# An attention, low-rank mix and MLP kernel on one core: float32 in the low-rank part, an earlier decode of two weight blocks, and the last first-layer products one part ahead

## The chip, the cores and the metric

The kernel runs on one core of a Trainium2 chip. The metric is device time in microseconds (us) of one execution; of the kernel before, three runs were timed, and a fourth execution was profiled. The engines are PE (TensorE matmuls; PEld are its weight loads), DVE (VectorE), ACT (ScalarE), POOL (GpSimd) and SP, which issues DMAs.

## What is computed

```python
# attention: batch 4, 12 heads, 448 tokens, head size 64
scores = q @ k.T / 8, causal mask, softmax
x = softmax @ v                      # (4, 448, 768)
# low-rank mix over the tokens, rank 32
u = x + ((x.T @ U) @ V).T            # U (448, 32), V (32, 448)
# MLP, 768 -> 3072 -> 768
out = u + relu(u @ w_ch1) @ w_ch2
```

The weights U, V, w_ch1 and w_ch2 come as float64 and are turned into float32 on the chip ("decoded").

## The kernel before, in words

Everything is held transposed: features on the partitions, tokens along the columns. There are three stages.

**Attention** (span 0 to about 152 us alone, then mixed with the next stage). A plan (`PLAN`, L47) lists the steps of a head with a lag each; iteration n does, in the plan's order, the scores of head n (tile `s`, L214), the transposes of its probabilities (`t`, L266) two iterations later, the product with v for each two heads (`pv`, L281), and so on. ACT takes exp (L242) and copies transposes out of PSUM (L167), DVE the row maxima (L228), POOL the normalising (L255). The instruction order in this stage and the next is the order in which the code is written (`manual_schedule`).

**The low-rank part** follows for each two heads: x is transposed back (`xt`, L311) and split into a high part, rounded to fp32r by ACT (`xn_h`, L315), and a low part, the rest, by DVE (`xn_l`, L320). For each four heads `low_rank` (`y`, L328) multiplies four tiles of 112 tokens with U: eight fp32r matmuls of 256 columns, with the high and low parts of U side by side in 128 weight columns (`um_s`). ACT copies the high part of y out (L337), DVE the low part (L341). `mix` (`hm`, L346 and L347) multiplies y with the high and the low part of V, two fp32r matmuls of 448 columns, for each of the six feature chunks of a batch; the mixes of batch 0 stand in iterations 14 to 19, those of batch 1 in 26 to 31. `mix_sum` (L351) adds on DVE. For batches 0 and 1 POOL then splits u into high and low parts (L171, L175). There are 12 `y` groups and 24 `hm` pairs in all: `y` in iterations 8, 12, ... 52.

**Decode.** A block of weights (128 x 768 float64, 768 KB) is loaded by SP (`load_w`) and decoded in three steps: step 0 has two ACT instructions (L152, L156) and three on DVE (L153 to L155), step 1 one on POOL (L160) and a DMA that keeps the result in HBM, step 2 a copy on ACT (L178) and a subtraction on DVE (L179). Blocks 0 and 1 are loaded in iterations 10 and 11 and decoded in iterations 26 to 32 (`W_AT` counts back from `START` = 34); U and V are loaded after iteration -1 and decoded in iterations 3, 5 and 6 (`VU_AT`).

**MLP of batches 0 and 1** (152 to 580 us): `hf` (L415) and `of` (L440), in groups of 9 fp32r matmuls, with the rest of attention, the low-rank steps and the decode of the other blocks put between them.

**MLP of batches 2 and 3** (580 us to the end): a Strassen scheme with 7 products for each quad of weight blocks, all at L647, in six parts p. A part has the first-layer quads (1, p, 0) and (1, p, 1), 63 matmuls each, and three second-layer quads (2, p, k), 42 each; a pair (q, n) in the code is product n of quad q, in PSUM banks `sa`, `sb` and `se`. When a first-layer quad is done, `hidden` turns its result r into seven operands with high and low parts (`h`): for each of r's halves and sums ACT rounds to the high part (L469) and DVE subtracts (L461). Second-layer results are added to x by DVE (`xb<-sa` and so on, L461). The order of the products is written by hand (`seq`); within it a scheduler places the instructions of this stage on the engines. Tiles `uch` and `ucl` hold the operands of the first layer to the end.

Of the kernel before, what the change touches and what calls it, by code (L numbers as in the profile page):

```python
# [69 lines left out]
def attention_mix_mlp(ctx: ExitStack, tc: tile.TileContext, qk, v, w1, w2, vu, out):  # L70
# [42 lines left out]
    um_s = const.tile([CP, NT, 4, R], F32R, name="um_s")  # L113
    vm_h = const.tile([P, S], F32R, name="vm_h")
    vm_l = const.tile([P, S], F32R, name="vm_l")
    xn_h = const.tile([CP, NT, 2 * P], F32R, name="xn_h")
    xn_l = const.tile([CP, NT, 2 * P], F32R, name="xn_l")
# [63 lines left out]
    def low_rank_weights(step):  # L181
        if step == 0:
            st["vu"] = load_words(vu, VCOLS)
        elif step == 1:
            st["vua"] = decode_bits(st["vu"], VCOLS)
        elif step == 2:
            decode_sum(st.pop("vu"), st["vua"], VCOLS)
        else:
# [1 line left out]
            split(a[:, :S], vm_h, vm_l)  # L190
            u = a[:CP, S:].rearrange("p (s r) -> p s r", s=NT)
            for i in (0, 2):
                split(u, um_s[:, :, i, :], um_s[:, :, i + 1, :])
# [539 lines left out]
    for p in range(NPART):  # L733
# [4 lines left out]
        else:  # L738
            order((b, 0), (b, 1), (k2, 5), (b, 2), (b, 3), (b, 4))
        if p + 1 < NPART:  # L740
# [3 lines left out]
            order((k1, 0), (k1, 3))  # L744
        else:
            order((b, 5), (b, 6), (k0, 0, 0), (k0, 3, 0), (k0, 1, 0), (k1, 0, 0), (k1, 3, 0), (k1, 1, 0))
            order((k0, 0, 1), (k0, 3, 1), (k0, 2), (k0, 1, 1), (k0, 6), (k0, 4), (k1, 0, 1), (k1, 3, 1))
        order((k0, 5), (k1, 2))
        order(*([(k1, 1)] if p + 1 < NPART else [(k1, 1, 1)]), (k1, 6), (k1, 4))
# [229 lines left out]
```

## Time and profile before

| | |
|---|---|
| runs | 911.19, 913.18, 915.44 us; median 913.18 us |
| profiled execution | 909.54 us, of it span 907.6 us |
| PE busy in the span | 877.9 us, 97% |
| DVE, ACT, POOL busy | 663.6, 486.6, 314.4 us (73%, 54%, 35%) |
| chain that ended last | PE 78%, DVE 10%, ACT 7% |

The profile page shows one execution; its views by stretches, by groups of instructions and in order of time are shown below. A matmul's record lasts longer than the array is held by it, since matmuls are pipelined: the price of a group is read from its start to the start of what follows.

### The profile page before, as it was taken

To read this page: it belongs to the slowest core of one execution; us is meant where nothing else is said; L and a number is where in the kernel's file an instruction comes from. 1 tells how busy PE (TensorE), PEld (TensorE's weight loads), DVE (VectorE), ACT (ScalarE), POOL (GpSimd) and SP (SyncE) were. 2 spreads that over 40 slices of the span, in tenths; PEclk is the share of its full clock that TensorE was granted. 3 is DMA by queue.
4 is the path that set the end of the run, shared out by engine and by line. 5 is a ranking of instruction groups with operands and counts; after the bars stand their busy time and mean duration, and the time that the engine had idled before them with its cause. 6 is when DMAs were issued, how large, how long until landed. Compare 5 with 4: busy or idle time off the path is not lost.

```text
span 907.6 us, 13761 instructions
## 1 busy us (share of the span) xinstructions
PE 877.9 (97%) x4728; PEld 749.6 (83%) x4728; DVE 663.6 (73%) x1320; ACT 486.6 (54%) x1050; POOL 314.4 (35%) x342
## 2 busy tenths in 40 slices
PE   6999998999999999999999999899999998999998
PEld 4776766888888888878889999898999897898987
DVE  4656677565665756657568788789888988989885
ACT  5998987654555544455444545364453634445350
POOL 3547576221222322223214425323424323322420
PEclk9999999999999999999999999999999999999999
DMA  8584565354454455433434446612211321202103
GB/s 209 135 216 128 151 156 155 125 174 139 135 179 134 157 165 163 139 116 119 153 105 156 157 157 208 203 42 71 70 52 35 94 59 42 72 24 85 47 1 122
DMA packets 51285, 110.02 MB, mean 121 GB/s; under 512 B 5392, under 2 KB 26896, under 8 KB 51216
## 3 DMA queue, kind: packets, MB, share of 16 engines
q1 hardware_dynamic: 51216, 109.14, 39.7%
q8 instruction: 38, 0.62, 0.3%
q14 instruction: 31, 0.25, 0.1%
HBM read 84.74 MB, written 24.38 MB: 120 GB/s over the span
## 4 chain that ended last, share of the span: by engine, by line
PE 78%; DVE 10%; ACT 7%; issue 3%; DMA 1%; POOL 1%; SPq 0%; DVEq 0%; ACTq 0%; POOLq 0%
PE hf L415 20%; PE of L440 19%; PE sa L647 14%; PE se L647 6%; PE s L214 5%; PE pv L281 5%; PE t L266 4%; ACT p L242 3%; PE sb L647 3%; DVE h L461 2%; DVE tmp L461 2%; DVE sw L461 1%; DVE wsp L461 1%; PE y L328 1%; DVE p L228 1%
## 5 line engine op out<-in xcount | busy, mean ns | idle before, releaser
L440 PE MATMUL of<-g,wsp 128*128 128x448 f32 x864 | 183.8, 368 | 0.0
L461 POOL TENSOR_TENSOR wsp<-wld,wsp 128x512 fp32r<-128x512 f32 (+1 forms) x60 | 104.1, 1745 | 219.2 <-ACT wsp L584 113.2
L440 PEld LDWEIGHTS of<-g,wsp 128*128 128x128 f32 x864 | 160.2, 188 | 18.3 <-issue 2.1
L160 POOL TENSOR_TENSOR wa<-wld 128x768 int32<-128x768 int32 (+1 forms) x49 | 73.2, 1494 | 289.0 <-issue 159.6
L242 ACT ACTIVATE p<-p,m 112x448 f32<-112x448 f32 x192 | 99.7, 523 | 59.6 <-DVE m L228 59.3
L255 POOL TENSOR_SCALAR p<-p,r 112x448 f32<-112x448 f32 x192 | 96.7, 521 | 67.7 <-DVE r L250 40.5
L647 PE MATMUL sa<-h,wsp 128*128 128x448 f32 x432 | 98.5, 367 | 1.4 <-DVE xb L461 0.7
L647 PE MATMUL sa<-uch,wsp 128*128 128x448 f32 x288 | 89.6, 371 | 7.5 <-ACT r L668 4.8
L415 PE MATMUL hf<-u,wsp 128*128 128x448 f32 x432 | 94.9, 370 | 0.0
L415 PE MATMUL hf<-wsp 128*128 128x448 f32 x432 | 94.0, 368 | 0.5 <-ACT pt L167 0.5
L228 DVE CUSTOM_DVE_ANT_0 p<-s,mask 112x448 f32<-112x448 f32 x192 | 75.8, 443 | 20.0 <-PE s L214 19.1
L443 DVE TENSOR_TENSOR xa<-of,xa 128x448 f32<-128x448 f32 x96 | 58.7, 619 | 42.9 <-PE of L440 42.3
L647 PEld LDWEIGHTS sa<-h,wsp 128*128 128x128 f32 x432 | 80.7, 188 | 9.9 <-DVE xb L461 2.0
L415 PEld LDWEIGHTS hf<-u,wsp 128*128 128x128 f32 x432 | 79.8, 188 | 10.7 <-issue 3.8
L415 PEld LDWEIGHTS hf<-wsp 128*128 128x128 f32 x432 | 80.0, 188 | 9.9 <-issue 0.9
L424 DVE SCALAR_TENSOR_TENSOR g<-hf,g 128x448 fp32r<-128x448 f32 x48 | 29.9, 623 | 71.9 <-ACT g L423 71.8
L214 PE MATMUL s<-qk 64*112 64x448 f32 (+3 forms) x384 | 70.5, 444 | 6.6 <-DMA qk<-in_qk_dram 4.2
L178 ACT CAST wsp<-wa 128x768 fp32r<-128x768 f32 x48 | 40.0, 833 | 68.4 <-POOL wa L160 50.9
L423 ACT ACTIVATE g<-hf 128x448 fp32r<-128x448 f32 x48 | 26.1, 543 | 84.0 <-PE hf L415 83.8
L167 ACT COPY pt<-t 112x336 f32<-112x336 f32 x144 | 62.1, 472 | 10.7 <-PE t L266 10.7
L647 PEld LDWEIGHTS sa<-uch,wsp 128*128 128x128 f32 x288 | 54.0, 188 | 16.2 <-ACT r L668 8.3
L584 ACT CAST wsp<-wld 128x512 fp32r<-128x512 f32 (+1 forms) x60 | 41.7, 703 | 47.1 <-PE sa L647 35.7
(92 smaller groups left out, 1598.4 us busy)
## 6 DMA issues: line engine op xcount, KB each, us to landing
wld<-in_w_dram SPq DMA_DIRECT2D x48, 768.0 KB, 4.7
qk<-in_qk_dram SPq DMA_DIRECT2D x96, 224.0 KB, 4.1
kept<-wa SPq DMA_DIRECT2D x48, 384.0 KB, 2.6
wld<-kept SPq DMA_DIRECT2D x24, 384.0 KB, 3.3
wld<-kept SPq DMA_DIRECT2D x72, 128.0 KB, 2.5
v<-in_v_dram SPq DMA_DIRECT2D x24, 224.0 KB, 4.8
out_dram<-xa SPq DMA_DIRECT2D x12, 224.0 KB, 2.3
out_dram<-xb SPq DMA_DIRECT2D x12, 224.0 KB, 1.9
```

The costliest lines, as they stand in the source:

```text
L160: nc.gpsimd.tensor_tensor(a.bitcast(I32), t[:, :n, 1].bitcast(I32), t[:, :n, 0].bitcast(I32), op=ALU.add)
L167: nc.scalar.copy(o, i)
L214: nc.tensor.matmul(o[:, : (i + 1) * CP], t[r, 0, i * CP : (i + 1) * CP], t[r, 1, : (i + 1) * CP], start=True, stop=True,)
L228: nc.vector.tensor_tensor_reduce(out=st["p", b, h][:, POFF[i] : POFF[i] + n], in0=st.pop(("o", b, h, i))[:, :n], in1=mask[:, S - n :], sca ...
L242: nc.scalar.activation(pi, pi, AF.Exp, bias=m[:, i : i + 1], scale=-1.0, accum_out=l[:, i : i + 1])
L255: nc.gpsimd.tensor_scalar(pi, pi, r[:, i : i + 1], 1.0, op0=ALU.mult, op1=ALU.mult)
L281: nc.tensor.matmul(o[j * D : (j + 1) * D, kt * CP : S], v[:, kt, j, :], pt[:, n0 : n0 + S - kt * CP], start=(kt == 0), stop=(kt == NT - 1),)
L415: nc.tensor.matmul(o, a[:, cs], m, start=(kc + n == 0), stop=(kc + n == NC + 1))
L440: nc.tensor.matmul(o, a[:, cs], m, start=(fc + n == 0), stop=(fc + n == FC + 1))
L443: nc.vector.tensor_tensor(x, o, x, op=ALU.add)
L461: (nc.vector if e == "V" else nc.gpsimd).tensor_tensor(o, a, b, op=op)
L647: nc.tensor.matmul(st[bank, q], a, b, start=(n in FIRST and ms[0] == 0 and k == 0), stop=(n in LAST and end and k == len(steps) - 1), skip ...
```

## The change

Three things are changed.

1. The low-rank part is float32 throughout. U, V, x and y have no low parts: two DVE copies in place of three splits, `natural_low` (DVE, 24 instructions) and `low_rank_low` (DVE, 12) are gone, and `y` has 32 rows. `low_rank` has four float32 matmuls of 256 columns with 32 weight columns in place of eight fp32r ones, `mix` one float32 matmul of 448 columns over 32 rows in place of two fp32r ones over 128 rows. A float32 matmul of the code is two instructions in a trace: the program has two `pv` products of 448 columns for each two heads, the trace four.
2. U and V are loaded after iteration 1 and decoded in iterations 4 to 6; blocks 0 and 1 are loaded in iterations 3 and 5 and decoded in iterations 8 to 13.
3. In the Strassen stage the quad (1, 5, 1) of the last part is multiplied in part 4, among that part's second layer. Both first-layer quads of part 5 then go through `hidden` at the end of part 4, into tiles that held `uch` and `ucl`; part 5 has second-layer products alone. The last quad's results are stored as each is ready in the code's order.

```diff
-VU_AT = (-1, 3, 5, 6)
+VU_AT = (1, 4, 5, 6)
-W_AT = (8, 6, 4, 3, 2)
+W_AT = (8, 9, 10, 11, 13)
...
     def low_rank(b, n):
         if n == 0:
-            st["y", b] = p_y.tile([P, DM], F32R, tag="y", name="y")
-        o = st["yo", b, n] = bank("y")[:, : 2 * P]
+            st["y", b] = p_y.tile([R, DM], F32, tag="y", name="y")
+        o = st["yo", b, n] = bank("y")[:R, : 2 * P]
         for s in range(NT):
-            for t in (xn_h, xn_l):
-                nc.tensor.matmul(
-                    o,
-                    um_s[:, s].rearrange("p a r -> p (a r)"),
-                    t[:, s, :],
-                    start=(s == 0 and t is xn_h),
-                    stop=(s == NT - 1 and t is xn_l),
-                )
...
+            nc.tensor.matmul(o, um[:, s], xn[:, s, :], start=(s == 0), stop=(s == NT - 1))
...
-    def low_rank_low(b, n):
-        y, o = st["y", b][D:, n * 2 * P : (n + 1) * 2 * P], st.pop(("yo", b, n))
-        nc.vector.tensor_tensor(y, o[D:], f(y), op=ALU.subtract)
...
     def mix(b, c):
         o = st["h", b, c] = bank("hm")[:, :S]
-        ys = st["y", b][:, c * P : (c + 1) * P]
-        nc.tensor.matmul(o, ys, vm_h, start=True, stop=False)
-        nc.tensor.matmul(o, ys, vm_l, start=False, stop=True)
+        nc.tensor.matmul(o, st["y", b][:, c * P : (c + 1) * P], vm, start=True, stop=True)
...
         def operand(key):
+            if q[1] == NPART - 1:
+
+                if not last:
+                    last.extend(p_uc.tile([P, 7, S], F32R, tag=f"u{x}{k}", name="h") for x in "hl")
...
+        if p + 2 == NPART:
+
+            b2 = (1, p + 1, 1)
+            order((a2, 0), (b, 5), (a2, 1), (b, 6), (a2, 2), (a2, 3))
+            order((k0, 0, 0), (k0, 3, 0), (a2, 4), (k0, 1, 0), (a2, 5), (k0, 0, 1), (k0, 3, 1), (a2, 6))
+            order((k0, 2), (k0, 1, 1), (b2, 0), (k0, 4), (b2, 1), (k0, 6), (b2, 2), (k0, 5), (b2, 3), (b2, 4))
+            order((k1, 0), (b2, 5), (k1, 3), (b2, 6), (k1, 2), (k1, 1), (k1, 6), (k1, 4))
...
-                    if q[0] == 2 and q[2] == NC // 2 - 1 and q[1] + 1 < NPART:
+                    if q[0] == 2 and q[2] == NC // 2 - 1 and q[1] + 2 < NPART:
                         layer.extend(hidden((1, q[1] + 1, 0)))
+                    elif q == (1, NPART - 1, 1):
+                        layer.extend(hidden((1, NPART - 1, 0)) + hidden(q))
...
-        early += [(10, load_w, (0,)), (11, load_w, (1,))]
+        early += [(3, load_w, (0,)), (5, load_w, (1,))]
```

On PE, iteration 16: the scores, `y`, `xt` and `hm`. Before:

```order
L214 MATMUL s<-qk 112x224
L328 MATMUL y<-xn_h,um_s 128x256
L328 MATMUL y<-xn_l,um_s 128x256
L328 MATMUL y<-xn_h,um_s 128x256
L328 MATMUL y<-xn_l,um_s 128x256
L328 MATMUL y<-xn_h,um_s 128x256
L328 MATMUL y<-xn_l,um_s 128x256
L328 MATMUL y<-xn_h,um_s 128x256
L328 MATMUL y<-xn_l,um_s 128x256
L311 MATMUL xt<-ident,xa 112x128 x4
L346 MATMUL hm<-vm_h,y 128x448
L347 MATMUL hm<-vm_l,y 128x448
```

And now, in the same iteration:

```order
L210 MATMUL s<-qk 112x224
L318 MATMUL y<-xn,um 32x256 x4
L307 MATMUL xt<-ident,xa 112x128 x4
L325 MATMUL hm<-vm,y 128x448
L262 MATMUL t<-ident,p 112x112 x10
```

The places stay; eight matmuls have become four, and two have become one.

On ACT, step 0 of the decode of block 0 (the two rows from `wld`) stands between a head's exps and its copies. Before, in iteration 26:

```order
L242 ACTIVATE p,l<-p,m 112x448
L242 ACTIVATE p,l<-p,m 112x336
L242 ACTIVATE p,l<-p,m 112x112
L242 ACTIVATE p,l<-p,m 112x224
L152 ACTIVATE wa<-wld 128x768
L156 ACTIVATE wld<-wld 128x768
L167 COPY xa<-pv 128x448
L167 COPY pt<-t 112x336
```

Now, in iteration 8:

```order
L238 ACTIVATE p,l<-p,m 112x448
L238 ACTIVATE p,l<-p,m 112x336
L238 ACTIVATE p,l<-p,m 112x112
L238 ACTIVATE p,l<-p,m 112x224
L150 ACTIVATE wa<-wld 128x768
L154 ACTIVATE wld<-wld 128x768
L165 COPY xa<-pv 128x448
L165 COPY pt<-t 112x336
```

The two instructions stand at the same place of an iteration that is 18 earlier.

On DVE, the work around the last `hidden`. Before, in part 5, where (1, 5, 1) is turned into operands:

```order
L461 TENSOR_TENSOR r<-se,r 128x448
L461 TENSOR_TENSOR h<-r,h 128x448
L461 TENSOR_TENSOR tmp<-r 128x896
L461 TENSOR_TENSOR r<-se,r 128x448
L461 TENSOR_TENSOR h<-tmp,h 128x896
L461 TENSOR_TENSOR tmp<-r,tmp 128x448 x2
L461 TENSOR_TENSOR h<-r,h 128x896
L461 TENSOR_TENSOR xb<-se,xb 128x448
L461 TENSOR_TENSOR h<-tmp,h 128x896
L461 TENSOR_TENSOR xb<-sa,xb 128x448
L461 TENSOR_TENSOR xb<-sb,xb 128x448
L461 TENSOR_TENSOR wsp<-sw,wsp 128x512
```

Now, at the end of part 4, in the middle of the two quads (1, 5, 0) and (1, 5, 1):

```order
L439 TENSOR_TENSOR tmp<-r,tmp 128x448
L439 TENSOR_TENSOR xb<-se,xb 128x448
L439 TENSOR_TENSOR xb<-sa,xb 128x448
L439 TENSOR_TENSOR h<-tmp,h 128x896
L439 TENSOR_TENSOR h<-r,h 128x896
L439 TENSOR_TENSOR tmp<-r 128x896
L439 TENSOR_TENSOR xb<-sa,xb 128x448
L439 TENSOR_TENSOR h<-r,h 128x448
L439 TENSOR_TENSOR h<-tmp,h 128x896
L439 TENSOR_TENSOR xb<-se,xb 128x448
L439 TENSOR_TENSOR tmp<-r,tmp 128x448
L439 TENSOR_TENSOR xb<-sa,xb 128x448
```

Before, one quad's operands stand there with one addition between them; now two quads' operands follow each other, with the additions of part 4's second layer between them. From the first `h<-r,h 128x896` of the two quads to the addition that the last product of part 4, n = 5 of (2, 4, 2), waits for (it frees bank `sa`), DVE's order has 27 rows: six `h` of 896 columns, two `h` of 448, one `tmp<-r` of 896 columns, four `tmp<-r,tmp`, eleven additions to `xb`, one to `r` and two weight steps (`wsp<-sw`). In the same stretch PE's order has 91 matmuls between the last one of (1, 5, 1) and that product.

## Rows read from the trace of the kernel before

**Rows 1.** Busy time by stretches: start and end in us, length, then busy us and instructions of PE, PEld, DVE, ACT and POOL, the granted clock of PE, DMA share and GB/s. Iterations 8 to 13, the MLP stage with attention in it, and the last part.

```profile
35.37:59.84 24.47, 24.20 (x187) 19.07 (x185) 14.12 (x67) 22.66 (x75) 11.57 (x24) 1.00 0.76 201
...
152.00:470.00 318.00, 315.98 (x1699) 264.44 (x1700) 196.61 (x402) 159.25 (x327) 80.97 (x98) 1.00 0.45 142
...
861.00:907.60 46.60, 41.00 (x195) 35.67 (x193) 33.29 (x54) 13.44 (x24) 8.61 (x6) 0.99 0.16 60
```

**Rows 2.** The same view by pairs of iterations, each from one `pv` group to the next: two pairs of batch 0 with mixes in them, two of batch 1 with mixes and decode, and what follows.

```profile
59.84:68.69 8.85, 8.79 (x63) 6.37 (x61) 5.55 (x25) 8.26 (x28) 4.79 (x10) 1.00 0.72 161
...
77.80:86.45 8.65, 8.58 (x61) 5.79 (x60) 5.51 (x24) 7.58 (x25) 6.97 (x13) 1.00 0.52 133
...
110.52:121.42 10.90, 9.03 (x62) 6.35 (x61) 8.15 (x28) 9.85 (x30) 6.08 (x10) 1.00 0.44 118
...
130.53:141.42 10.89, 8.84 (x61) 5.82 (x61) 8.85 (x23) 9.03 (x26) 8.65 (x16) 1.00 0.65 148
141.42:152.00 10.58, 10.34 (x66) 6.89 (x65) 8.32 (x27) 7.57 (x26) 7.46 (x10) 0.84 0.55 170
```

**Rows 3.** PE in order of time in iteration 16: start, length, line, operation, tiles, shape.

```profile
72.96 0.39 PE L328 MATMUL y<-xn_h,um_s 112*128 112x256 f32 x1
...
74.02 0.60 PE L311 MATMUL xt<-ident,xa 128*112 128x128 f32 x4
74.38 0.45 PE L346 MATMUL hm<-vm_h,y 128*128 128x448 f32 x1
...
74.87 1.12 PE L266 MATMUL t<-ident,p 112*112 112x112 f32 x10
```

**Rows 4.** PE in order of time in the MLP stage, around the last low-rank groups.

```profile
440.84 0.28 PE L328 MATMUL y<-xn_h,um_s 112*128 112x256 f32 x1
...
441.80 2.00 PE L415 MATMUL hf<-wsp 128*128 128x448 f32 x9
...
454.47 2.09 PE L415 MATMUL hf<-u,wsp 128*128 128x448 f32 x9
456.40 0.60 PE L311 MATMUL xt<-ident,xb 128*112 128x128 f32 x4
...
457.25 2.01 PE L415 MATMUL hf<-u,wsp 128*128 128x448 f32 x9
459.10 0.36 PE L346 MATMUL hm<-vm_h,y 128*128 128x448 f32 x1
...
459.50 1.99 PE L415 MATMUL hf<-wsp 128*128 128x448 f32 x9
...
468.44 0.44 PE L346 MATMUL hm<-vm_h,y 128*128 128x448 f32 x1 [1.53 <-DVE y L341]
```

**Rows 5.** PE groups by line and shape in the first 150 us: count, busy us, mean ns of one.

```profile
L281 PE MATMUL pv<-pt,v 112*64 112x448 f32 x60 | 18.1, 584 | 1.4 <-ACT pt L167 1.2
...
L281 PE MATMUL pv<-pt,v 112*64 112x112 f32 x60 | 7.8, 268 | 0.0
...
L328 PE MATMUL y<-xn_l,um_s 112*128 112x256 f32 x28 | 7.0, 281 | 0.0
...
L347 PE MATMUL hm<-vm_l,y 128*128 128x448 f32 x12 | 4.4, 366 | 0.0
```

**Rows 6.** DVE in order of time at the last `y` of the kernel: the subtraction that `hm` of Rows 4 waits for.

```profile
467.86 0.43 DVE L341 TENSOR_TENSOR y<-y 64x256 fp32r<-64x256 f32 x1
```

**Rows 7.** ACT groups by line and shape between 110.52 and 141.42 us: the decode's instructions.

```profile
L156 ACT ACTIVATE wld<-wld 128x768 int32<-128x768 uint32 x2 | 1.8, 909 | 0.0
L152 ACT ACTIVATE wa<-wld 128x768 f32<-128x768 f32 x2 | 1.8, 888 | 0.0
...
L178 ACT CAST wsp<-wa 128x768 fp32r<-128x768 f32 x1 | 0.8, 818 | 0.0
```

**Rows 8.** DVE in order of time: one decode instruction in iteration 30.

```profile
133.65 2.50 DVE L179 TENSOR_TENSOR wsp<-wa,wsp 128x768 fp32r<-128x768 f32 x1
```

**Rows 9.** DVE and ACT groups by line and shape from 809 to 905 us, the last two parts.

```profile
L461 DVE TENSOR_TENSOR xb<-sa,xb 128x448 f32<-128x448 f32 x25 | 15.4, 620 | 6.1 <-PE sa L647 6.0
L461 DVE TENSOR_TENSOR h<-tmp,h 128x896 fp32r<-128x896 f32 x8 | 11.8, 1479 | 1.5 <-ACT h L469 1.5
...
L461 DVE TENSOR_TENSOR tmp<-r,tmp 128x448 f32<-128x448 f32 x8 | 6.4, 797 | 0.6 <-DVE tmp L461 0.5
L461 DVE TENSOR_TENSOR h<-r,h 128x896 fp32r<-128x896 f32 x3 | 4.3, 1436 | 0.0
...
L461 DVE TENSOR_TENSOR tmp<-r 128x896 f32<-128x896 f32 x3 | 3.2, 1082 | 0.0
L461 DVE TENSOR_TENSOR h<-r,h 128x448 fp32r<-128x448 f32 x4 | 3.2, 795 | 1.2 <-ACT h L469 1.2
...
L469 ACT CAST h<-r 128x896 fp32r<-128x896 f32 x3 | 2.8, 944 | 0.0
```

**Rows 10.** PE in order of time in part 5: its two longest stops.

```profile
873.87 0.36 PE L647 MATMUL sa<-uch,wsp 128*128 128x448 f32 x1
875.00 0.47 PE L647 MATMUL se<-uch,wsp 128*128 128x448 f32 x1 [0.77 <-DVE r L461]
...
879.78 0.37 PE L647 MATMUL se<-h,wsp 128*128 128x448 f32 x1
880.81 0.47 PE L647 MATMUL sa<-h,wsp 128*128 128x448 f32 x1 [0.66 <-ACT h L469]
```

More of the change, by code (lines that the diff above doesn't have):

```diff
@@ L112, in attention_mix_mlp @@
     mask = const.tile([CP, S], F32, name="mask")
[L113 to L117, printed above, removed]
+    um = const.tile([CP, NT, R], F32, name="um")
+    vm = const.tile([R, S], F32, name="vm")
+    xn = const.tile([CP, NT, 2 * P], F32, name="xn")
     def f(ap):
@@ L189, in low_rank_weights @@
             a = f(st.pop("vua"))
[L190 to L193, printed above, removed]
+            nc.vector.tensor_copy(vm, a[:R, :S])
+            nc.vector.tensor_copy(um, a[:CP, S:].rearrange("p (s r) -> p s r", s=NT))
     def load_qk(b, h):
@@ L641, in product @@
             else:
-                bh, bl = st["H", m][j]
+                bh, bl = st["H", q[1], m][j]
             cs = slice(m * P, (m + 1) * P)
@@ L696, in hidden @@
         ops = [None] * 7
+        last = []
         def operand(key):
+            if q[1] == NPART - 1:
+                if not last:
+                    last.extend(p_uc.tile([P, 7, S], F32R, tag=f"u{x}{k}", name="h") for x in "hl")
+                h, l = (t[:, UPOS[key]] for t in last)
+                for n in [2] if key == "o" else range(UPOS[key].start, UPOS[key].stop):
+                    ops[n] = last[0][:, n], last[1][:, n]
+                return h, l
             if key == "o":
@@ L712, in end @@
         def end():
-            st["H", k] = ops
+            st["H", q[1], k] = ops
             used.add(("H", q[1], k))
@@ L743, in attention_mix_mlp @@
             order((a2, 5), (k0, 0, 1), (k0, 3, 1), (a2, 6), (k0, 2), (k0, 1, 1), (k0, 6), (k0, 4))
-            order((k1, 0), (k1, 3))
+            order((k1, 0), (k1, 3), (k0, 5), (k1, 2), (k1, 1), (k1, 6), (k1, 4))
         else:
[L746 to L749, printed above, removed]
+            order((k0, 0), (k0, 3), (k2, 5), (k0, 2), (k0, 1), (k0, 6), (k0, 4), (k1, 0), (k1, 3))
+            order((k0, 5), (k1, 2), (k1, 1), (k1, 6), (k1, 4))
         order((k3, 0), (k3, 3), (k1, 5), (k3, 2), (k3, 1), (k3, 6), (k3, 4))
@@ L759, in attention_mix_mlp, with stored @@
             units.append(g)
-    def stored(q):
+    def stored(q, n):
         if q[0] == 2 and q[1] == NPART - 1:
-            for d in range(2):
-                for b in range(2):
-                    nc.sync.dma_start(
-                        out=out[2 * q[2] + d, :, (b + 2) * S : (b + 3) * S], in_=xs(q, d, b)
-                    )
+            for d, b in {1: ((0, 0),), 4: ((1, 1),), 5: ((0, 1),), 6: ((1, 0),)}.get(n, ()):
+                nc.sync.dma_start(
+                    out=out[2 * q[2] + d, :, (b + 2) * S : (b + 3) * S], in_=xs(q, d, b)
+                )
     loaded, prepared = [0], [0]
@@ L820, in strassen @@
                 results(q, n)
+                stored(q, n)
                 used.add((q, n))
@@ L853, in attention @@
             "lv": load_v, "v": values, "vc": values_out,
-            "xp": x_natural, "xh": natural_high, "xl": natural_low,
+            "xp": x_natural, "xh": natural,
         }
-        by_four = {"lp": low_rank, "lh": low_rank_high, "ll": low_rank_low}
+        by_four = {"lp": low_rank, "lh": low_rank_out}
         todo = []
@@ L897, in attention_mix_mlp @@
         ):
-            early += [(START - n, step, a) for step, a in steps]
+            early += [(n, step, a) for step, a in steps]
+        early.sort(key=lambda e: e[0])
         todo = attention()
```

17 lines of the change are left out of this document (6 added, 11 removed), and 4 rows, old and new, of the table PLAN.

## The prediction

> **What bounds the kernel now.** I read the stretches first [rows 1]. From 152 to 470 us PE is busy 315.98 of 318.00 us: whatever is added to PE there is paid in full, and whatever leaves DVE (196.61 us busy) or ACT (159.25 us) brings nothing unless PE was waiting for it. In iterations 8 to 13 PE is busy 24.20 of 24.47 us, but ACT stands at 22.66 us, so two engines are near the end of their time. In the last part DVE has 33.29 of 46.60 us and PE stops for short waits. Next the pairs of iterations [rows 2]: with two mixes and no decode a pair takes 8.85 and 8.65 us, with decode 10.90 and 10.89 us at the same PE work, and the stretch behind it runs at a mean granted clock of 0.84, that is, in part at 1.2 GHz instead of 2.4 GHz; before it, PE had stopped several times. Then single groups, start to start, for prices [rows 3, 4].
>
> **Part 1, float32.** What is removed on DVE (36 subtractions) is off the path but for one place: the last `y` is subtracted only at 467.86 us [rows 6], behind a decode's DVE work, and PE waits 1.53 us for it [rows 4]. That wait goes: -1.5 us. What is late next there is ACT's copy of y, which was long done.
>
> What is added is PE time. A float32 product is two instructions. Per instruction, the `pv` groups of 448 and 112 columns last 584 and 268 ns, which is 316 / 336 = 0.94 ns a column with the queueing in it; fp32r, with 366 ns at 448 columns and 281 ns at 256, takes 85 / 192 = 0.44 ns [rows 5]. 0.44 ns is about one column in a cycle at 2.4 GHz (0.417 ns). I take float32 as two cycles, 0.83 ns, for each of the two instructions: it lies below the 0.94 ns that hold some waiting for the neighbour head, and the lower bound is 0.44 ns, if the narrow shapes (32 weight columns, 32 rows) ran as fp32r does.
>
> - `y` after: 4 products x 2 instructions x 256 columns x 0.83 = 1.71 us (0.90 to 1.93). Before: 74.02 - 72.96 = 1.06 us in attention [rows 3], 441.80 - 440.84 = 0.96 us in the MLP stage [rows 4].
> - `hm` after: 2 x 448 x 0.83 = 0.75 us (0.39 to 0.84). Before: 74.87 - 74.38 = 0.49 us [rows 3], 459.50 - 459.10 = 0.40 us [rows 4].
> - A group of nine fp32r matmuls takes 456.40 - 454.47 = 1.93 us behind a float32 group and 459.10 - 457.25 = 1.85 us behind an fp32r one [rows 4]: 0.08 us more for what stands behind each new float32 group.
>
> From 152 us on there are 5 `y` and 12 `hm`: 5 x 0.75 + 12 x 0.35 + 17 x 0.08 = 9.3 us, less the 1.5 us: **+7.8 us**. In attention there are 7 `y` and 12 `hm`. The `hm` stand in iterations 14 to 19 and 26 to 31, where PE sets the pace: 12 x 0.26 = 3.1 us. Of the `y`, those of iterations 8 and 12 fall where ACT will set the pace (part 2) and are counted at nothing; if ACT has room they cost 0.65 us each. The other five: 3.3 us. Together **+6.4 us**. Both come to +14.2 us.
>
> The price of a column is the number on which this rests, so I set the skill beside it. In the rows one product costs 2 x 0.83 = 1.67 ns a column against 0.44 ns, 3.8 times. The Trainium skill, page "FP8 and Floating Point Precision", section "TensorE Precision Notes", says that true FP32 is four passes through the array. By that rule a column costs 4 x 0.44 = 1.76 ns and the 23,040 columns of all `y` and `hm` products 2 us more than in my sum; the trace agrees that the change's float32 is not free.
>
> **Part 2, the decode.** In its old place it cost (10.90 + 10.89) - (8.85 + 8.65) = 4.3 us [rows 2], and behind it the half clock: the `pv` group at 141.42 us belongs to the stretch at 0.84, whose missing 0.16 x 10.58 us is 1.7 us [rows 2]. Both go: -6.0 us. In its new place each step 0 adds two ACT instructions of about 0.9 us, and one copy of 0.82 us belongs to it: 2 x 1.8 + 0.8 = 4.4 us [rows 7], queued behind a head's exps and ahead of the copies that `t`, `pv` and PE wait for. ACT had 24.47 - 22.66 = 1.8 us of idle time there [rows 1], so the stretch grows by 2.6 us at least and 4.4 us at most; I take 3.5 us. On DVE and POOL the place is better: in iteration 30 a subtraction took 2.50 us [rows 8] while POOL was splitting u, and POOL does no splitting in iterations 8 to 13. SP is passed by two loads of 768 KB earlier than before; in iterations 8 to 13 the two loads stood in a DMA share of 0.76 without stopping PE [rows 1], so I cost them at nothing; if the loads of q and k behind them come late, it is the few us of a landing. U and V one iteration later in the decode: nothing, the same ACT work. Sum **-2.5 us** (-6.0 to +2).
>
> **Part 3, the last part.** It removes the wait for (1, 5, 1) in part 5. PE's two stops there are 875.00 - 873.87 and 880.81 - 879.78 us, each less the 0.2 us of a matmul: 0.92 + 0.82 = 1.7 us [rows 10]. It adds, at the end of part 4, two quads' operands in a row. DVE's order there has, from the first `h` to the addition that frees bank `sa` for part 4's last product, 6 `h` of 896 columns (2 x 1.44 + 4 x 1.48 = 8.8 us), 2 `h` of 448 (1.6), one `tmp<-r` (1.1), four `tmp<-r,tmp` (3.2), 12 additions of 0.62 (7.4) and two weight steps at about the same (1.2): 23.3 us [rows 9]. It can't begin before ACT's first cast of 0.94 us [rows 9], and that waits until PE has read the tiles `uch` for the last time. So the addition ends some 24.2 us after the last first-layer matmul. PE has 91 matmuls in that time, at 1.85 / 9 = 0.206 us each [rows 4]: 18.7 us. PE waits the difference, 5.5 us, in several stops, each at an addition that stands behind an `h`. Net **+3.8 us** (-1.7 if the stops vanish, +6 if DVE is slowed by POOL besides). The stores gain nothing: one of them waits for the last addition either way.
>
> **Sum.** 7.8 + 6.4 - 2.5 + 3.8 = +15.5 us. Against the profiled execution's 909.54 us that is 925.0 us; the median of the runs lies 3.6 us higher, at 913.18 us, and I forecast for it **928.7 us**, slower by 1.7%.
>
> **The rivals.**
>
> - *Float32 at fp32r's rate.* If an instruction of these narrow shapes takes 0.44 ns a column, the 46,080 columns of all instructions save 0.39 x 46,080 = 18.0 us: 910.7 us, no change. Against it: `pv`, with 64 weight columns, is narrow too and pays 0.94 ns.
> - *The narrow products run beside their neighbours* (the one on the other side). They take 12 x 1.71 + 24 x 0.75 = 38.5 us of PE. If more than 20.1 us of that lay beside other matmuls, the kernel would be faster by over 0.5%; with all of it hidden, 928.7 - 38.5 = 890 us. Against it: next to them stand `t`, `xt`, `hf` and `of` on 112 or 128 rows [rows 3, 4], which leave no rows free, and their own instructions use the same rows. The Trainium skill, page "TensorE: Matmul & The Clock Gate", section "Why this matters for your kernels", says that a matmul of 32 rows alone takes as long as one of 128 and that the gain lies in running it beside others in other row groups. No run here shows that for these shapes.
> - *Part 4 covers the operands.* PE's stops of 5.5 us don't come: 923.2 us. For it: a part holds two `hidden` of some 7.9 us of DVE each [rows 9] all along, and most of that is covered. Against it: DVE's order, counted above.
> - *The decode is free in its new place*: 925.2 us. For it: ACT idles 1.8 us there and DVE 10 us [rows 1], so a decode spread over six iterations may find most of its room. Against it: it needs 4.4 us of ACT.
> - *The decode and the loads hurt more*: ACT pays 4.4 us, a load comes one landing late and a stretch at half clock remains (1.7 us): about 934 us.
>
> **How the numbers follow.** The forecast 0.42; fp32r's rate 0.05; beside the neighbours 0.04; part 4 covered 0.20; decode free 0.15; more hurt 0.14. The range reaches from 916 us (part 4 covered, the decode free, and somewhat cheaper float32: 928.7 - 5.5 - 3.5 - 4) to 936 us (float32 at 0.94 ns a column, 5 us, or the last rival, and 2 us). A measurement of this kernel can tell about 0.5%, 4.6 us, from no change. Faster by more: 0.04, the second rival. Within: 0.06, the first rival and a little of the others. Slower by more: 0.90.
>
> **What would show it.** Right: `y` at 1.7 us and `hm` at 0.75 us, start to start; PE still at 99% from 152 to 470 us and that stretch longer by 8 us; pairs of iterations 26 to 31 near 9.5 us without stops; ACT over 95% busy in iterations 8 to 13; PE stops of some 5 us in all around the end of part 4, each ended by `xb` or `h` on DVE. Wrong: `y` near 1 us, or float32 groups that overlap others, which takes away 14 us; a stretch of iterations 8 to 13 as short as before; or no stops at the end of part 4.

## The result, and the profile of the changed kernel

Device time, medians of the runs made together:

| | before | changed |
|---|---|---|
| median of the runs, us | 913.15 (911.19 to 915.44, 4 runs) | 922.54 (921.92 to 923.26, 4 runs) |
| profiled execution, us | 909.54 | 922.83 |
| its span, us | 907.6 | 921.1 |
| ratio of the runs | 1 | 1.0102, 95% interval 1.0077 to 1.0127 |

The changed kernel is slower by 1.0%, 9.4 us by the medians and 13.5 us by the two profiled spans. The forecast was 928.7 us, 15.5 us more: the sign and the range held, and 6 us of the forecast size did not come.

The stretches and pairs that answer to [rows 1] and [rows 2], in the same columns: iterations 8 to 13, the MLP stage from the first `hf` to the last `hm`, then four pairs of iterations (14/15, 18/19, 26/27, 30/31) and the one up to the MLP stage.

```profile
34.23:63.82 29.59, 26.34 (x185) 18.67 (x185) 17.79 (x68) 27.16 (x82) 18.25 (x27) 1.00 0.58 160
155.89:487.67 331.78, 330.81 (x1704) 263.27 (x1702) 190.41 (x387) 158.62 (x327) 79.55 (x97) 1.00 0.42 135
...
63.82:72.86 9.04, 9.04 (x62) 5.66 (x60) 5.34 (x26) 8.13 (x27) 4.62 (x11) 1.00 0.95 250
83.67:92.72 9.05, 9.05 (x61) 5.66 (x60) 4.93 (x25) 7.76 (x25) 5.64 (x11) 1.00 0.48 127
118.21:127.25 9.04, 9.04 (x62) 5.66 (x60) 5.33 (x26) 8.12 (x27) 4.37 (x10) 1.00 0.48 127
138.07:147.11 9.04, 9.04 (x62) 5.66 (x61) 4.92 (x25) 7.75 (x25) 5.62 (x11) 1.00 0.49 129
147.11:157.91 10.80, 10.80 (x74) 7.58 (x73) 5.16 (x27) 9.06 (x30) 8.64 (x15) 1.00 0.48 118
```

Four things are to be seen. Iterations 8 to 13, which now hold the decode, take 29.59 us in place of 24.47, with ACT busy for 27.16 us of them. The pairs 26/27 and 30/31 went from 10.90 and 10.89 us to 9.04 us and now look like their twins of batch 0: PE is busy all the time, and the granted clock behind them is 1.00 where it was 0.84. The twins themselves, which had no decode, went from 8.85 and 8.65 us [rows 2] to 9.04 us: that is float32. And the MLP stage, 318.87 us from its first `hf` to its last `hm` before, takes 331.78 us with PE as full as it was.

The last low-rank groups, in order of time on PE, against [rows 4] (start, length, then line, operation, tiles, shape):

```profile
470.73 0.65 PE L307 MATMUL xt<-ident,xb 128*112 128x128 f32 x4 [0.62 <-ACT xb L165]
471.13 2.10 PE L393 MATMUL hf<-u,wsp 128*128 128x448 f32 x9
473.16 1.01 PE L325 MATMUL hm<-vm,y 32*128 32x448 f32 x2
474.10 2.09 PE L393 MATMUL hf<-wsp 128*128 128x448 f32 x9
476.13 1.01 PE L325 MATMUL hm<-vm,y 32*128 32x448 f32 x2
477.07 1.91 PE L318 MATMUL y<-xn,um 112*32 112x256 f32 x8
478.92 2.12 PE L393 MATMUL hf<-wsp 128*128 128x448 f32 x9
```

From start to start a `hm` takes 474.10 - 473.16 = 0.94 us (0.40 before), a `y` 478.92 - 477.07 = 1.85 us (0.96 before), and the nine `hf` between two `hm` 2.03 us (1.85 before). The 1.53 us for which PE waited for DVE's subtraction of `y` are gone. A new wait of 0.62 us stands at the `xt`: in the new order it follows its own `pv` directly and waits for ACT's copy; that `pv`, at 467.10 us, lasts 3.63 us to the `xt`, where the `pv` before (452.43 us) took 2.04 us to the `hf` behind it.

### The profile page after: what moved, and what is told of

It reads as the page before. It is cut to its first block, busy times and chain, and to the rows that moved or that the text cites. A ratio compares the mean times of both kernels' runs of the same rounds, so it can differ in the third digit from the quotient of the medians.

```text
span 921.1 us, 13723 instructions
## 1 busy us (share of the span) xinstructions
PE 899.6 (98%) x4728; PEld 744.1 (81%) x4728; DVE 644.2 (70%) x1283; ACT 488.0 (53%) x1047; POOL 313.7 (34%) x342
## 4 chain that ended last, share of the span: by engine, by line
PE 84%; DVE 7%; ACT 5%; issue 2%; DMA 1%; POOL 0%; SPq 0%; ACTq 0%; DVEq 0%; POOLq 0%
PE of L418 20%; PE hf L393 19%; PE sa L625 14%; PE se L625 7%; PE s L210 5%; PE pv L277 5%; PE t L262 4%; PE sb L625 4%; PE hm L325 2%; ACT p L238 2%; PE y L318 2%; DVE h L439 2%; DVE tmp L439 1%; PE xt L307 1%; DVE xb L439 1%
## 5 line engine op out<-in xcount | busy, mean ns | idle before, releaser
L210 PE MATMUL s<-qk 64*112 64x224 f32 (+3 forms) x384 | 67.9, 442 | 4.5 <-DMA qk<-in_qk_dram 4.2
L625 PEld LDWEIGHTS sa<-uch,wsp 128*128 128x128 f32 x288 | 54.0, 188 | 11.7 <-ACT r L646 6.6
L562 ACT CAST wsp<-sw 128x256 fp32r<-128x256 f32 (+3 forms) x60 | 34.0, 578 | 55.2 <-DVE sw L439 25.6
```

The source lines that it names most:

```text
L210: nc.tensor.matmul(o[:, : (i + 1) * CP], t[r, 0, i * CP : (i + 1) * CP], t[r, 1, : (i + 1) * CP], start=True, stop=True,)
L625: nc.tensor.matmul(st[bank, q], a, b, start=(n in FIRST and ms[0] == 0 and k == 0), stop=(n in LAST and end and k == len(steps) - 1), skip ...
```

## The experiments

"Stage" below means a difference of starts in a profiled execution: attention from the first `pv` to the first `hf`, MLP from there to the last `hm` group, then from it to the first `sa`, then to the end (the Strassen part). Medians are those of all runs made.

| run | us, median (lowest to highest, runs) | before in the same session, median us | ratio, 95% interval |
|---|---|---|---|
| e1 float32 alone | 925.59 (925.05 to 926.31, 4) | 911.05 | 1.0166, 1.0153 to 1.0179 |
| e2 decode alone | 902.44 (901.86 to 903.58, 4) | 911.05 | 0.9913, 0.9900 to 0.9926 |
| e3 part ahead alone | 910.88 (909.56 to 914.20, 12) | 911.05 | 1.0004, 0.9990 to 1.0017 |
| e4 decode and part ahead | 903.00 (902.38 to 906.64, 6) | 911.05 | 0.9923, 0.9908 to 0.9938 |
| e5 other bank | 908.49 (907.26 to 911.40, 8) | 910.82 | 0.9973, 0.9960 to 0.9987 |
| e6 e4 + `hm` float32 | 917.97 (917.29 to 918.31, 4) | 910.82 | 1.0075, 1.0058 to 1.0092 |
| e7 e4 + bank order of e5 + `y` float32, wide | 916.57 (915.05 to 918.94, 4) | 910.82 | 1.0063, 1.0041 to 1.0084 |
| e8 changed + second `hm` product | 942.83 (942.75 to 943.38, 4) | 910.82 | 1.0348, 1.0329 to 1.0368 |
| e9 e5 - two products | 906.24 (905.40 to 908.09, 5) | 911.20 | 0.9943, 0.9923 to 0.9963 |
| e10 e4 + two products | 905.77 (904.41 to 906.49, 5) | 911.20 | 0.9935, 0.9915 to 0.9955 |
| e11 e4, decode spread | 908.45 (906.60 to 910.02, 11) | 911.20 | 0.9968, 0.9952 to 0.9984 |
| e12 e4, decode in the middle | 911.74 (909.16 to 913.02, 12) | 911.20 | 0.9995, 0.9980 to 1.0010 |

### The three parts, each alone

e1 takes the low-rank lines of the diff and nothing else, e2 its numbers for the decode, e3 its part of the Strassen stage, e4 all but the low-rank lines (each shown by one or two of its lines):

```diff
 # e1
...
-        nc.tensor.matmul(o, ys, vm_h, start=True, stop=False)
-        nc.tensor.matmul(o, ys, vm_l, start=False, stop=True)
+        nc.tensor.matmul(o, st["y", b][:, c * P : (c + 1) * P], vm, start=True, stop=True)
...
 # e2
-VU_AT = (-1, 3, 5, 6)
+VU_AT = (1, 4, 5, 6)
...
-W_AT = (8, 6, 4, 3, 2)
+W_AT = (8, 9, 10, 11, 13)
...
 # e3
...
+            b2 = (1, p + 1, 1)
...
```

> The kernel before with the low-rank part in float32 and nothing else. By the reading of the changed kernel's trace (a y group 1.84 us, an hm group 0.94 us, both with some 0.1 us at each end that nothing covers): 12 y and 24 hm groups cost 17 us more (14 to 20). By the prediction's sizes (y 1.71, hm 0.75 us): 14.2 us more. If the price lies in the columns alone it ends at the second number, if the ends of the groups count too at the first.

> The kernel before with the first two blocks' decode in iterations 8 to 13 and the low-rank weights' decode one step later, and nothing else. By the reading of the trace (start 1.1 us shorter, iterations 8 to 13 3.5 us longer, the late iterations and the stretch at half clock 7.8 us shorter): 4.5 us less (2 to 7). By the prediction: 2.5 us less. Rival, the late decode hid behind TensorE anyway: no change or up to 3.5 us more.

> The kernel before with the last first-layer quad multiplied in part 4 and the stores of the last quads per product, and nothing else. By the prediction: 3.8 us more (5.5 us of stops around the end of part 4, 1.7 us removed from part 5). By the reading of the trace (stops of parts 4 and 5 as large in sum as before): 0 to 1.5 us less. By the rival that part 4 covers the operands: 1.7 us less.

> The changed kernel with the low-rank part as in the kernel before (high and low parts in fp32r): decode and part ahead only. By the reading of the trace: 5 to 6 us less than before. By the prediction's sizes (-2.5 and +3.8): 1.3 us more. If the parts add up, it stands against before at the sum of the two runs of these parts alone.

Measured: +14.5, -8.6, -0.2 and -8.1 us. The part ahead is worth nothing that these runs can tell (the interval is 1.5 us wide to either side). Float32 costs less and the moved decode brings more than expected. Stage by stage, attention and MLP of e1 are 6.5 and 12.8 us longer than before, those of e2 3.2 and 0.1 us shorter, so float32 costs 4.8 us less and the decode brings 5.3 us more than these two stages add up to. In both runs the way to the first `sa` is shorter by 2.1 and 2.8 us and the Strassen part by 2.1 and 2.0 us, though neither edit touches either. In e3 these two are as before; its profiled execution is the slowest of its 12 runs, so its attention and MLP are not compared. So 4 to 5 us hang on something that e1 and e2 both disturb. The parts don't add up either: 14.5 - 8.6 - 0.2 = 5.7 us, against 11.5 us by the changed kernel's median and the 911.05 us of before. A saving that e1 and e2 each make, and that the changed kernel can make only once, is counted twice in that sum.

### First accident: a PSUM bank

Before, PE reaches the Strassen part like this (order of time):

```profile
573.62 7.26 PE L440 MATMUL of<-g,wsp 128*128 128x448 f32 x35
583.45 0.45 PE L647 MATMUL sa<-uch,wsp 128*128 128x448 f32 x1 [2.57 <-DVE xa L443]
```

DVE's `xa` at L443 is the addition that reads the MLP's last `of`. In the built kernels of before and e3 that `of` lies in bank 0, and the first `sa` takes bank 0. In e1, e2, e4 and the changed kernel the rotation of the `ps` banks has shifted, and the last `of` lies in bank 5 or 7. The test leaves the rotation and the decode alone and gives `sa` another bank:

```diff
-        for bank, tag, n in (("a", f"A{i}", 1), ("b", "B", 2), ("e", f"E{i}", 1)):
+        for bank, tag, n in (("b", "B", 2), ("a", f"A{i}", 1), ("e", f"E{i}", 1)):
```

> The kernel before with one line changed: the psb tiles of the Strassen part are requested in the order b, a, e, so that the first sa product takes another PSUM bank than the one that the last of group has just filled. The decode stays in iterations 26 to 32. If the 2.57 us stop at 580.88 and the longer stop at the start of part 3 come from that bank, which float32 alone and decode alone had each moved by accident: 4.5 us less than before (3.5 to 5). If these stops were removed by the moved decode or by the shorter DVE work itself: no change.

```profile
570.26 10.29 PE L440 MATMUL of<-g,wsp 128*128 128x448 f32 x50
580.39 0.37 PE L647 MATMUL sa<-uch,wsp 128*128 128x448 f32 x1
```

The stop is gone in e5 (PE, order of time): 109.94 us from the last `hm` to the first `sa` as in e2, and 2.3 us less in all. That is half of what was expected. (In e11, where the decode stands elsewhere again, a stop of 0.98 us for the same addition is back.) The stop at the start of part 3 of the Strassen stage did not go: 3.15 us from matmul to matmul, 2.93 us before, 1.20 us in e1, e2 and e4. It has a second cause.

### Second accident: where a load of instructions falls

The wait at that stop ends with ACT's copy `r`, behind ACT's cast of a weight block that is read back by the four `wld<-kept` transfers. In e5, PE and ACT in order of time:

```profile
761.67 0.47 PE L647 MATMUL sa<-uch,wsp 128*128 128x448 f32 x1 [2.79 <-ACT r L668]
```

```profile
760.16 0.62 ACT L584 CAST wsp<-wld 128x512 fp32r<-128x512 f32 x1 [1.85 <-DMA wld<-kept]
```

The DMA view of the stretch around it, in e5: queues with packets, MB and share, then the issues with KB each and median us to landing:

```profile
q1 hardware_dynamic: 1228, 0.92, 52.6%
q8 instruction: 1, 0.02, 1.8%
issues: line engine op xcount, KB each, median us to landing
wld<-kept SPq DMA_DIRECT2D x4, 128.0 KB, 5.4
```

and in e4:

```profile
q1 hardware_dynamic: 1232, 0.92, 41.0%
issues: line engine op xcount, KB each, median us to landing
wld<-kept SPq DMA_DIRECT2D x4, 128.0 KB, 3.2
```

With one instruction packet on queue 8 among the reads, they land 2.2 us later. In all runs the long stop and that packet come together. Queue 8's packets are 16 KB, and around this stop in before they stand at the 8114th, 8359th and 8613th of PE's records: about 250 instructions apart. I take them for loads of PE's own program, since they keep their places in it: in e8, where PE comes to the stop some 95 records later, they stand at the 8097th, 8366th and 8629th. The stop stands at the 8369th in before. So I counted PE's instructions ahead of the first `sa` in the built kernels (a product as two, a float32 product of the low-rank part as four, and the instructions that only wait):

| kernels | instructions | stop at part 3, us |
|---|---|---|
| changed, e1 | 5885 | 1.33, 1.20 |
| e2, e4 | 5887 | 1.20, 1.20 |
| before, e3, e5, e7 | 5889 | 2.93, 2.66, 3.15, 3.11 |
| e6 | 5893 | 3.10 |
| e8 | 5982 | 1.26 |

From 5889 to 5893 the stop is long; with 93 more, in e8, it is short again, as it has to be if the load moves on with the program and leaves the reads. Two runs test it from both sides: e5 with four instructions fewer (two low-by-high products of one hidden group left out, so its output lacks a small term), and e4 with four more (two products of 64 columns into unused columns of a hidden group's bank):

```diff
 # e9, on e5
...
+                            if (p, k, b, n) == (1, 0, 0, 2) and kc in (1, 2):
+                                continue
 # e10, on e4
...
+                    o = bank("hf")
+                    if (p, k, b) == (1, 0, 0):
+                        for _ in range(2):
+                            nc.tensor.matmul(
+                                o[:, S:], wh[:, :P], st["u", b, 0][0][:, : 512 - S],
+                                start=True, stop=True,
+                            )
+                    o = o[:, :S]
...
```

> The kernel before with the psb tiles requested in the order b, a, e (908.5 us, stop of 3.15 us at the start of part 3), and with two low-by-high products of one hidden group left out, which shortens TensorE's program ahead of the Strassen part by four instructions. If the stop is long because a 16 KB load of TensorE's own instructions falls among the reads of the weight blocks, and where it falls is set by the number of instructions ahead: the load comes after the stop, the reads land in some 3.3 us in place of 5.4, the stop is 1.2 us, and the kernel is 2.3 us shorter (2 to 4; 0.4 of it the work left out). If the length of the stop has another cause: 0.4 us shorter, stop still near 3 us.

> Decode and part ahead without float32 (903.0 us, stop of 1.20 us at the start of part 3), with two extra products of 64 columns into the unused columns of one hidden group's bank: four more TensorE instructions ahead of the Strassen part, 0.1 us of work. If the place of the instruction load sets the stop: near 3 us in place of 1.20, and the kernel 1.9 to 4 us longer (the upper end where the clock falls after the stop). If not: 0.1 us longer.

PE at the stop in e9, in order of time, and the reads:

```profile
760.81 0.47 PE L649 MATMUL sa<-uch,wsp 128*128 128x448 f32 x1 [0.87 <-ACT r L670]
```

```profile
wld<-kept SPq DMA_DIRECT2D x4, 128.0 KB, 3.3
```

The same two views in e10:

```profile
758.63 0.48 PE L654 MATMUL sa<-uch,wsp 128*128 128x448 f32 x1 [2.36 <-ACT r L675]
```

```profile
q8 instruction: 1, 0.02, 1.3%
issues: line engine op xcount, KB each, median us to landing
wld<-kept SPq DMA_DIRECT2D x4, 128.0 KB, 4.1
```

Four instructions turn the stop off (1.23 us in place of 3.15, kernel 2.3 us shorter than e5) and on (2.72 us in place of 1.20, kernel 2.8 us longer than e4); the Strassen part of the profiled executions is 1.8 us shorter and 1.2 us longer. In e11 and e12, with 5887 and 5886, it is 1.20 and 1.15 us. In e6 and e7 the stop brought a second loss: the clock fell behind it. Windows of e6, columns as in [rows 1]:

```profile
767.30:770.50 3.20, 0.46 (x3) 0.09 (x2) 2.06 (x4) 1.58 (x4) 0.89 (x1) 0.90 0.03 6
770.50:776.50 6.00, 6.00 (x16) 5.35 (x17) 2.69 (x5) 2.50 (x5) 1.65 (x2) 0.50 0.00 0
776.50:780.00 3.50, 3.50 (x18) 3.18 (x18) 1.07 (x2) 1.17 (x3) 0.00 (x0) 0.98 0.00 0
```

At a granted clock of 0.50, the lower of the two levels (1.2 GHz), PE made 16 matmuls in 6.0 us; at 0.98 it made 18 in 3.5 us.

### The price of float32

```diff
 # e6, on e4: y in fp32r, its two sums of 32 rows kept as 64 rows of float32
-        nc.tensor.matmul(o, ys, vm_h, start=True, stop=False)
-        nc.tensor.matmul(o, ys, vm_l, start=False, stop=True)
+        nc.tensor.matmul(o, ys, vm, start=True, stop=True)
...
 # e7, on e4 and the banks of e5: y in float32 with 128 weight columns, U, 0, U, 0
-    um_s = const.tile([CP, NT, 4, R], F32R, name="um_s")
+    um_s = const.tile([CP, NT, 4, R], F32, name="um_s")
...
 # e8, on the changed kernel (and the banks of e5)
-        nc.tensor.matmul(o, st["y", b][:, c * P : (c + 1) * P], vm, start=True, stop=True)
+        ys = st["y", b][:, c * P : (c + 1) * P]
+        nc.tensor.matmul(o, ys, vm, start=True, stop=False)
+        nc.tensor.matmul(o, ys, vz, start=False, stop=True)
...
```

> Decode and part ahead as in the changed kernel, y in fp32r with high and low parts as before, hm alone one float32 product with 64 weight rows. Base: the same without float32, 903.0 us. By the reading of the trace (an hm group 0.94 us): 24 groups at 0.40 to 0.53 more, 9.5 us more than the base, 912 to 913. By the prediction's size of 0.75 us: 7.3 more, 910.

> Decode and part ahead as in the changed kernel, hm in fp32r as before, y alone in float32 with 128 weight columns in place of 32 (two of the four groups of columns are zero). Base 903.0 us. By the reading of the trace (12 groups at 0.89 more, some 3 us hidden in the iterations that wait for ACT): 7 to 10 us more, 910 to 913. If the number of weight columns plays no part the y group takes 1.84 us as with 32; if narrow products are cheaper it takes clearly longer than 1.84.

> The changed kernel with a second float32 product in each hm group, against a tile of zeros with the same weights (and the psb tiles requested in the order b, a, e). If the price of an hm group is 0.75 us of columns and 0.19 us at its two ends, the group takes 1.69 us and the kernel 18 us more than the changed one, 940. If each product carries its own 0.19 us, the group takes 1.88 us and the kernel 22.5 us more, 945.

The times of e6 and e7, 15.0 and 13.6 us over e4, hold the second accident (Strassen stages 4.0 and 3.1 us longer), and e7 2.1 us more on the way to the first `sa`: the 540 matmuls there start 206.7 ns apart in place of 202.7, with no wait among them, and why they do stays open. Attention and MLP alone: e6 +3.0 and +8.9 us, e7 +4.1 and +7.9, the changed kernel, with both, +7.1 and +12.9. In attention that is the sum; in the MLP stage it is 3.9 us less than the sum, and PE's waits there differ by about as much: 2.0 us in e4, 2.7 in e6 and 4.9 in e7, but 1.0 in the changed kernel.

In e8 a group of two `hm` products lasts 497.82 - 496.12 = 1.70 us (PE in order of time):

```profile
496.12 1.01 PE L328 MATMUL hm<-vm,y 32*128 32x448 f32 x2
496.98 0.91 PE L329 MATMUL hm<-vz,y 32*128 32x448 f32 x2
497.82 2.09 PE L397 MATMUL hf<-u,wsp 128*128 128x448 f32 x9
```

The second product adds 0.76 us, its columns alone, and the 0.19 us stand once per group. The kernel came 20.3 us over the changed one, between the 18 and the 22.5 us; the trace decides for the first: the 24 groups are 18 us, and the way to the first `sa` is 2.1 us longer by the same slower spacing as in e7 (206.7 ns). In e6 a `hm` takes 0.95 us with 64 weight rows as with 32. In e7 the number of weight columns did play a part. PE in order of time, a `y` of e7 in the MLP stage:

```profile
290.85 1.89 PE L322 MATMUL y<-xn,um_s 112*128 112x256 f32 x8
292.38 2.19 PE L409 MATMUL hf<-wsp 128*128 128x448 f32 x9
294.41 0.60 PE L311 MATMUL xt<-ident,xb 128*112 128x128 f32 x4
```

and the same of the changed kernel:

```profile
296.57 1.91 PE L318 MATMUL y<-xn,um 112*32 112x256 f32 x8
298.41 2.09 PE L393 MATMUL hf<-u,wsp 128*128 128x448 f32 x9
300.34 0.38 PE L307 MATMUL xt<-ident,xb 128*112 128x128 f32 x2
```

`y` and the nine `hf` behind it take 294.41 - 290.85 = 3.56 us with 128 columns and 300.34 - 296.57 = 3.77 us with 32. In e4, with fp32r, they take 2.78 us. The wide float32 `y` thus costs 0.78 us, close to what the forecast had (0.75 + 0.08); the narrow one 0.21 us more. In single records the load of the next weights begins together with the last instruction of the wide `y` and 0.31 us after the start of the last one of the narrow `y`. My expectation that the width plays no part fell.

### Another place for the decode

```diff
-W_AT = (8, 9, 10, 11, 13)
+W_AT = (17, 18, 21, 29, 31)      # e11
+W_AT = (16, 17, 19, 20, 22)      # e12
```

> Decode and part ahead without float32, with the decode steps in iterations 17, 18, 21, 29 and 31 in place of 8 to 13. In the pairs of iterations 8 to 13 ACT had 0.6 us idle of 8.2, so that the decode's 4.0 us of ACT work lengthened them by 4.6 us; the pairs 16/17, 20/21 and 28/29 have 1.1 us idle each. If ACT's idle time sets the price: some 1.2 us in place of 4.6, the kernel 3 us shorter than the base of 903.0 (2 to 4). If the decode costs the same wherever it stands, by DVE and GpSimd waits: no change or up to 3 us longer, as in the old place.

> As the run before it, with the decode in iterations 16, 17, 19, 20 and 22. ACT's two decode_bits steps stand in pairs with 1.1 us idle and the copies of one block in one more: by ACT's idle time some 1.5 us in place of 4.6, 2.5 to 3 us shorter than 903.0. If it costs the same wherever it stands: no change.

Both are slower than e4, by 5.5 and 8.7 us, and the attention stage says it as well: 131.44 us in e4, 135.80 in e11, 141.65 in e12, where the granted clock was 0.50 for 6.8 us behind the first decode step of each block (from 79.7 and 103.6 us). ACT's idle time does not set the price; that theory fell. The traces point to DVE and POOL instead. DVE in order of time in e12, such a first step in iterations 16/17:

```profile
71.81 2.09 DVE L153 TENSOR_SCALAR wa<-wa 128x768 f32<-128x768 f32 x1
73.94 1.38 DVE L154 TENSOR_SCALAR wa<-wa 128x768 uint32<-128x768 uint32 x1
75.36 1.19 DVE L155 SCALAR_TENSOR_TENSOR wld<-wld,wa 128x768 uint32<-128x768 uint32 x1
```

POOL at the same time:

```profile
71.58 1.92 POOL L255 TENSOR_SCALAR p<-p,r 112x448 f32<-112x448 f32 x4 [1.21 <-PE t L266]
73.46 1.45 POOL L175 TENSOR_TENSOR wsp<-xa,wsp 128x448 fp32r<-128x448 f32 x1
```

and DVE in e4, the same step in iteration 8:

```profile
39.65 0.83 DVE L153 TENSOR_SCALAR wa<-wa 128x768 f32<-128x768 f32 x1 [0.41 <-ACT wa L152]
40.52 0.78 DVE L154 TENSOR_SCALAR wa<-wa 128x768 uint32<-128x768 uint32 x1
```

and POOL beside it:

```profile
39.43 3.22 POOL L255 TENSOR_SCALAR p<-p,r 112x448 f32<-112x448 f32 x4 [1.70 <-DVE r L250]
```

With POOL idle, later in the kernel, L153 and L154 take 0.56 us and L179, one row per block, 0.95. In iterations 8 to 13 they take 0.83, 0.78 and 1.30 us, in e12's iterations 2.09, 1.38 and 2.49 (groups by line). POOL works beside them in both places, with the same four L255. What differs is who gives way: in e4 L153 ends 0.4 us after the first of the four, and the other three last 0.84, 0.75 and 1.05 us in place of 0.55, 0.45 and 0.36; in e12 it ends 0.4 us after the fourth, and the four lose nothing. L154 then meets the split of u (L175), which runs in iterations 15 to 21 and 27 to 33 and not in 8 to 13. The next head's maximum and, through it, PE's `t` wait behind them: 1.7 us in the pair 16/17 of e12, put down to DVE `m`. The Trainium skill, page "SBUF — State Buffer", section "SBUF: two separate sides", says that VectorE and GpSimd share a pair of ports which one instruction holds until it ends while the other is blocked. The trace agrees for single instructions, as above; that four of POOL's pass in a row while L153 stands is more than that, and what decides it stays open. That this is the whole price of the other places is argued from the durations: no run here moved POOL's work away from the decode.

The best versions that ran are the decode alone (e2) and the changed kernel without float32 (e4), 0.9 and 0.8% faster than before; in the stages that the edits don't touch, 4.8 and 4.6 us of that are the two accidents.

## Why the prediction was right, and where its sizes failed

| term | forecast, us | profiled executions, us |
|---|---|---|
| float32 from the MLP stage on | +7.8 | +14.0 (e4 to changed: 12.9 + 0.7 + 0.4) |
| float32 in attention | +6.4 | +7.1 (e4 to changed) |
| decode | -2.5 | -3.3 (before to e2, attention and MLP) |
| last part | +3.8 | +0.2 (e2 to e4, of 318.3 from the first `sa` to PE's last matmul; e3: -0.2 us by medians) |
| PSUM bank at the first `sa` | none | -2.8 (before to e2) |
| instruction load at part 3 | none | -2.0 (before to e2, Strassen part) |
| sum | +15.5 | +13.2 |

The measured terms add up to 13.2 us, the two spans differ by 13.5 us. The medians say 9.4 us because the profiled execution of before, 909.54 us, lies 3.6 us below its median of that session, and the changed one 0.3 us above; against the 910.8 to 911.2 us of the later sessions the difference is 11.3 to 11.7 us.

**Float32: the mechanism and the price of a column were right, the ends of a group were missed.** 0.76 us for a second `hm` product and 0.215 us from one 256-column instruction of `y` to the next are the 0.83 ns a column of the forecast. The step that failed here is the term "`y` after 1.71, `hm` after 0.75, 0.08 us for what stands behind", which priced a group by its columns: it measured 1.84, 0.94 and about 0.15. For 12 `y` and 24 `hm` the first two are 1.6 + 4.6 = 6.2 us more. In attention, shorter waits elsewhere covered most of it (the `s` groups take 3.6 us less in the changed kernel than in e4); in the MLP stage, at a full PE, nothing did. By e7, 0.2 us of each `y` is the price of 32 columns among full-width neighbours. That the 0.19 us of `hm` has the same cause is argued, not shown: its 32 and 64 rows were run, 128 rows in float32 were not. The Trainium skill, page "TensorEngine Tiling (Array Packing)", section "Key Properties", says that changing the tiling mode drains the engine; a loss at both ends of a narrow group and none inside it agrees with that: of the 0.94 us of a `hm`, its first instruction takes 0.48 and its second 0.46 us, where the columns alone are 0.37 each, and e8's second product adds nothing but columns. The rest of the excess is the `xt` behind its `pv`, 1.6 us, in the new order of the steps.

The four passes of the Trainium skill's page "FP8 and Floating Point Precision", section "TensorE Precision Notes", which the prediction weighed, would by its estimate have given 1.76 ns a column; the rows gave 0.215 x 2 / 256 = 1.68 ns. So the time that was missed lay at the ends of the groups and not in the columns.

**The decode: both halves were too small, the sum nearly right.** The old place cost 6.8 us (41.38 to 34.60 us from the `pv` at 110.52 us to the MLP stage, before to e2) where the forecast had 6.0; the new one 4.6 us in iterations 8 to 13, just above the 4.4 us that it gave as upper bound; and 1.0 us went ahead of them with the later decode of U and V. ACT was busy for 26.60 of the 29.07 us in e2, 92% and not over 95%: PE waited there for ACT's copies (2.0 us), for POOL's `p` (0.9 us) and for DVE's `y` (0.7 us).

**The last part: the step that failed is the 24.2 us for DVE against 18.7 us for PE.** The same 27 rows of DVE run from 873.54 to 893.81 us in the changed kernel, 20.3 us. The durations came from groups of the last two parts [rows 9], where some instructions run beside POOL (an `h` of 896 columns takes 1.08 us alone and 2.07 to 2.79 us when POOL is at work through most of it); at the end of part 4 all six run alone. DVE by shape from 872.5 to 892.5 us, and PE's two longest stops there:

```profile
L439 DVE TENSOR_TENSOR tmp<-r,tmp 128x448 f32<-128x448 f32 x4 | 4.5, 1124 | 0.0
L439 DVE TENSOR_TENSOR h<-tmp,h 128x896 fp32r<-128x896 f32 x4 | 4.3, 1082 | 0.0
...
L439 DVE TENSOR_TENSOR h<-r,h 128x896 fp32r<-128x896 f32 x2 | 2.2, 1089 | 1.0 <-ACT h L447 1.0
```

```profile
882.00 1.49 PE L625 MATMUL sa<-h,wsp 128*128 128x448 f32 x6 [0.81 <-DVE xb L439]
...
885.57 2.11 PE L625 MATMUL sa<-h,wsp 128*128 128x448 f32 x9 [0.26 <-DVE xb L439]
```

From start to start the six `h` take 6.0 us where the forecast had 8.8, the twelve additions 6.4 for 7.4, and the four `tmp<-r,tmp`, two of them beside POOL, 4.2 for 3.2; the rest is near its forecast. Nor did the 0.94 us of ACT's first cast stand behind PE's last read of `uch`: it began at 872.56 us, before that read (873.39 us). What is left of the stops is some 2 us, as much as part 5 lost: the rival that part 4 covers the operands was nearly right.

**What no rival held:** 4.8 us from two places that the diff doesn't touch. With the 3.6 us of the last part that didn't come and the 0.8 us that the decode brought more, they outweigh the 6.9 us of float32 that were missed. So the sign and the kind of cost were right by reasoning, and that the total came within 6 us was in part luck: errors of opposite sign.

## What to carry to other kernels

Price a product by its group, not by its columns: a float32 group on 32 rows or columns between full-size fp32r neighbours paid 0.2 us on top of 0.83 ns per column and instruction, and a `y` padded to 128 columns did not. Judge a place for DVE's elementwise work by what its instructions last beside POOL's there, not by ACT's gaps. And before a gain or loss of a few us is put down to an edit, compare the stages that the edit doesn't touch: a bank rotation and four instructions on PE moved this kernel by 2 to 3 us each, as much as the parts of the change.

## What the runs showed of the hardware that was not expected

- A 16 KB load of PE's own instructions among 128 KB reads delays their landing from 3.2 or 3.3 to between 4.1 and 5.4 us. Whether it falls there was set here by PE's instruction count ahead of the Strassen part: not up to 5887, in all six kernels from 5889 to 5893, and not with 5982. That PE's sequencer, running ahead, asks for the next block just before or just after it halts at this wait would explain it; that reading is argued only.
- Stops of about 3 us were followed by stretches at the lower clock in some executions (e6, e7: 6.8 and 3.4 us at 0.50 behind the stop at part 3) and not in others (before, e3, e5). What decides stays open.
